# An attention-and-mixer kernel: the first block's u transposed by DMAs that ScalarE issues, the third batch's x by DMA too, key beacons loaded first

## Chip, cores and metric

The kernel runs on one core of a Trainium2 chip. The metric is device time in microseconds of one execution; the kernel before takes 357.06 us (median of 3 runs, 356.78 to 357.49). Engines: TensorE (PE, matrix multiply; PEld is its weight load), VectorE (DVE), ScalarE (ACT), GpSimd (POOL) and SyncE (SP). PE writes only PSUM, which this kernel uses as eight tiles of one bank each. Data moves by DMAs, issued from a queue of POOL, SP or ACT.

## What is computed

```
# B, H, S, Nb, D = 8, 8, 576, 16, 64
k_all = concat([beacon_k, k]); v_all = concat([beacon_v, v])
a = softmax(q @ k_all^T / sqrt(D), causal on the S part)
x = (a @ v_all) as (B, S, H*D)              # 8 x 576 x 512
h = x^T @ U @ V                             # over the 576 tokens, rank 32
u = x + h^T
out = u + relu(u @ w_ch1) @ w_ch2           # 512 -> 2048 -> 512
```

So each batch first has attention (8 heads), then its tokens are mixed (u = x + low-rank term), then each token goes through two dense layers with a residual u.

## The kernel before

**Attention.** Heads go in pairs p (4 per batch, 32 in all). For the first four batches q and k are loaded by POOL's queue into `st` tiles (`token_load`, f32 to f16 on the way; the 16 beacon rows by `key_beacons`), regrouped by DVE into `pr` (L252, and L254 for the beacons), transposed on PE (L259), and copied by DVE into `qT` and `kT` (L292, L297). Later batches are loaded whole and turned by DMA transposes that SP issues (L607). Scores (L329) go to PSUM, ACT takes the exponentials into `expt` (L335), DVE masks (L305, L307), PE multiplies by v into `po` (L357), and DVE normalises into `xb` (L365, L366): x of the batch, tokens on partitions.

**Mixing.** `mix_units` makes uT, u transposed: channels on partitions, all 4,608 tokens in a row. `head` computes x^T U (qtp, L393), `most` and `end` multiply by V (L417, L429). In the form without turning, PE also adds x itself, by matmuls of xb with an identity (`x_into`, L372), and DVE and ACT copy the result out (L406, L408). In the turned form SP first issues five DMA transposes of xb into uT (L384) and DVE adds the matmul's result to them (L404). Batch 0 has a form of its own (`first_mix`), batches 1 and 2 go without turning, batches 3 to 7 are turned.

**Dense layers.** `mlp_units` works on blocks of 512 tokens (nine). A g unit is four matmuls (L487) and a relu on ACT (L500) or DVE (L502); a c unit is four matmuls (L512), sixteen of them to an output tile of 128 tokens. At the end u must be added, with tokens on partitions again. For block 0 PE does it, by four matmuls of uT with the identity for each output tile (L520), and ACT and DVE copy alternate tiles (L527, L529) to `ob`. For blocks 1 to 8, SP issues four DMA transposes of uT into `ut` (L481) at the block's first g unit, and DVE adds `ut` on the way out (L525). SP stores `ob` (L530).

**Order.** Each engine's order is the order of the program (a manual schedule), and each engine works strictly in its own order. Dense units wait in a list, `queue`, and `fill` takes them between attention's steps. `mix(b)` puts the mixing steps of batch b among the queued units: `head` after n units, `most` after k more and `end` three later. For batches 0 and 1 the loop over `NP1` pairs runs, with `FIRST` units per pair; then `fill(AHEAD - 8)`, two `regroup_of`, `fill(8)`, and the main loop. POOL's queue is the only one that loads tokens and weights, one after another; `load_batch` issues the loads of the next batch at the first pair of a batch.

Of the kernel before, what the change touches and what calls it, by code (L numbers as in the profile page):

```python
# [18 lines left out]
P = 128  # L19
# [11 lines left out]
def kernel(  # L31
# [13 lines left out]
    nc = tc.nc  # L45
    B, H, S, D = q.shape
# [6 lines left out]
    NH2 = H // 2  # L53
# [48 lines left out]
    def pst(shape, dtype, name):  # L102
        return psum.tile(shape, dtype, tag="ps", name=name)
# [41 lines left out]
    uT = const.tile([P, NCC, B * S], F16, name="uT", tag="uT")  # L145
# [42 lines left out]
    def beacon_load(eng, src, dst, hs):  # L188
        eng.dma_start(out=dst[0:Nb], in_=src[hs].rearrange("h p d -> p h d"))  # L189

    def token_load(eng, src, dst, hs):
        eng.dma_start(out=dst[0:TP, hs, :], in_=src[hs].rearrange("h (p j) d -> p h (j d)", j=TJ))

    def key_beacons(eng, src, dst, hs):
        beacon_load(eng, src, dst[TP:TB, hs, (TJ - 1) * D : TJ * D], hs)
# [15 lines left out]
    def v_loads(src, bsrc, vs):  # L211
        v_beacon(bsrc, vs)
        v_tokens(src, vs, ALLH)
# [4 lines left out]
    ALLH = slice(0, H)  # L218
# [6 lines left out]
        return st, whole  # L225

    def emit_loads(b, L, vs):
        token_load(nc.gpsimd, k[b], L[0][0], ALLH)
        token_load(nc.gpsimd, q[b], L[0][1], ALLH)
        key_beacons(nc.gpsimd, beacon_k[b], L[0][0], ALLH)  # L230
        v_loads(v[b], beacon_v[b], vs)


# [234 lines left out]

        return head, begin, rest

    def mlp_units(t0, n, dst, flip, turned=True, last=False):


        units = []
        gT = {}
        held = {}

        def turn():
            ut = utp.tile([P, 4, DM], F16, name="ut", tag="ut")
            for cc in range(NCC):  # L480
                nc.sync.dma_start_transpose(out=ut[:, :, ts(cc, P)], in_=uT[:, cc, ds(t0, 4 * P)])  # L481
            gT["u"] = ut

        def g_part(dc, upto):
            g, done = held.get(dc) or (pst([P, 512], F32, name="gps"), 0)
            for cc in range(done, upto):
                nc.tensor.matmul(  # L487
                    g[:, 0:n], w1[:, cc, ts(dc, P)], uT[:, cc, ds(t0, n)], start=(cc == 0), stop=(cc == NCC - 1)
                )
            held[dc] = g, upto  # L490

        def g_unit(dc):
            if dc == 0:
                gT["t"] = gtp.tile([P, NDC, 512], F16, name="gT", tag="gT")
                if turned:
                    turn()
            g_part(dc, NCC)
            g, _ = held.pop(dc)
            if (dc % 3 if not turned else (dc + flip) % 2 or dc in (5, 6, 7)):
                nc.scalar.activation(out=gT["t"][:, dc, 0:n], in_=g[:, 0:n], func=AF.Relu)  # L500
            else:
                nc.vector.tensor_scalar_max(out=gT["t"][:, dc, 0:n], in0=g[:, 0:n], scalar1=0.0)  # L502

        cps = {}

        def c_unit(i, part):
            m = min(P, n - P * i)
            if part == 0:
                cps["t"] = pst([P, DM], F32, name="cps")
            ps = cps["t"]  # L510
            for dc in range(4 * part, 4 * part + 4):
                nc.tensor.matmul(  # L512
                    ps[:m, :], gT["t"][:, dc, ds(P * i, m)], w2[:, dc, :], start=(dc == 0),
                    stop=turned and dc == NDC - 1, skip_group_check=True,
                )
            if part == 3:
                ob = outp.tile([P, DM], F32, name="ob", tag="ob")
                if not turned:
                    for cc in range(NCC):
                        nc.tensor.matmul(  # L520
                            ps[:m, ts(cc, P)], uT[:, cc, ds(t0 + P * i, m)], ident, start=False, stop=True,
                            skip_group_check=True,
                        )
                if turned:
                    nc.vector.tensor_tensor(out=ob[:m, :], in0=ps[:m, :], in1=gT["u"][:m, i, :], op=ALU.add)  # L525
                elif i % 2:
                    nc.scalar.activation(out=ob[:m, :], in_=ps[:m, :], func=AF.Copy)  # L527
                else:
                    nc.vector.tensor_copy(out=ob[:m, :], in_=ps[:m, :])  # L529
                nc.sync.dma_start(out=dst(i, m), in_=ob[:m, :])  # L530

        def c_half(i, part):
            hs = ds(DM // 2 * (part // 2), DM // 2)
            if part % 2 == 0:
                cps["t"] = pst([P, DM // 2], F32, name="cph")
            for dc in range(NDC // 2 * (part % 2), NDC // 2 * (part % 2 + 1)):
                nc.tensor.matmul(  # L537
                    cps["t"], gT["t"][:, dc, ts(i, P)], w2[:, dc, hs], start=(dc == 0), stop=(dc == NDC - 1)
                )
            if part % 2:  # L540
                ob = outp.tile([P, DM // 2], F32, name="oh", tag="ob")
                nc.vector.tensor_tensor(out=ob, in0=cps["t"], in1=gT["u"][:, i, hs], op=ALU.add)
                nc.sync.dma_start(out=dst(i, P)[:, hs], in_=ob)

        units += [lambda dc=dc: g_unit(dc) for dc in range(NDC)]
        for i in range((n + P - 1) // P):
            c = c_half if last and i == n // P - 1 else c_unit
            units += [lambda i=i, part=part, c=c: c(i, part) for part in range(4)]
        return units, g_part


    good = const.tile([P, B * H, NT], F16, name="good", tag="good")
# [21 lines left out]
    rows = out.rearrange("b s c -> (b s) c")  # L574
    NP = B * NH2
    NBLK = B * S // 512
    Ls, qTs, xbs = {}, {}, {}

    def load_batch(b):
        if b < DT0:  # L580
            Ls[b] = qk_tiles()
            emit_loads(b, Ls[b], vss[b % 2])
        else:
            v_loads(v[b], beacon_v[b], vss[b % 2])
# [52 lines left out]
    def regroup_of(p):  # L637
        b, c = divmod(p, NH2)
        prs[p] = [regroup(Ls[b][0], c, i, nc.vector.tensor_copy) for i in range(2)]
# [40 lines left out]
    NF = 2  # L680
# [4 lines left out]
    LAG = 10  # L685
# [7 lines left out]
    queue = []  # L693
    state = {"t": 0}
# [13 lines left out]
    def feed(b):  # L708

        while state["t"] < NBLK and 512 * (state["t"] + 1) <= S * (b + 1):  # L710
            t = state["t"]
            units, state["part"] = mlp_units(
                512 * t, 512, lambda i, m, t=t: rows[ds(512 * t + P * i, m), :], t % 2, t > 0, t == NBLK - 1
            )
            queue.extend(units)
            state["t"] += 1

    def mix(b):

        turned = b >= NF and len(queue) >= LAG + 7  # L720
        turn, head, parts = mix_units(xbs[b], S * b, turned)
        if turned:
            turn()
        n = (LAG + 3 * (b == B - 1)) if turned else 2 if b >= NF else 0
        k = 2 if turned else 1
        most, end = parts
        rest = queue[n + k + 3 :]
        queue[:] = queue[0:n] + [head] + queue[n : n + k] + [most] + queue[n + k : n + k + 3] + [end]
        for _ in range(4):
            queue.extend(rest[:1] + [None])  # L730
            del rest[:1]
        queue.extend(rest)
        feed(b)

    with tc.manual_schedule(engines={ENG.PE, ENG.Activation, ENG.DVE, ENG.SP, ENG.Pool}):
# [11 lines left out]
        t0, sc = qkT_of(0), scores_of(0)  # L747
# [41 lines left out]
        av = av_of(2)  # L789
        head, begin, rest = first_mix(xbs[0])  # L790
        feed(0)
        part = state["part"]
        D0, D1, D2 = range(3)
        av[0]()
        head(0, 2)
# [18 lines left out]
        t0, sc = qkT_of(4), scores_of(4)  # L814
# [14 lines left out]
        for p in range(NH2, NP1):  # L829
            b, c = divmod(p, NH2)  # L830
            if c == 0:
                load_batch(b + 1)
            seq = []
            masks = lambda: None
            if p + 2 < NP1:
                seq += [lambda i=i, p=p: qkT_of(p + 2)[i]() for i in range(2)]
            if p + 3 < NP1:
                seq.append(lambda p=p: regroup_of(p + 3))
            if p + 1 < NP1:
                seq.append(sc[1])  # L840
                masks = sc[2]
            seq += av_of(p)
            sc = []
            if p + 2 < NP1:
                new_qT_of(p + 2)
                sc = scores_of(p + 2)
                seq.append(sc[0])
            seq.append(masks)
            done = 0
            for i, u in enumerate(seq):  # L850
                u()
                want = FIRST[c] * (i + 1) // len(seq)
                fill(want - done)
                done = want
            if c == NH2 - 1:
                mix(b)
# [5 lines left out]
        t0, sc, t1 = qkT_of(NP1), scores_of(NP1), qkT_of(NP1 + 1)  # L862
# [5 lines left out]
        for p in range(NP1, NP):  # L868
            b, c = divmod(p, NH2)
# [83 lines left out]
    with tc.If(n_bad != 0, label="general"):  # L953
        with tc.For_i(0, B, 1) as bi:
            L = qk_tiles()
# [13 lines left out]
            for t0 in range(0, S, 512):  # L969
                n = min(512, S - t0)  # L970
# [32 lines left out]
```

## Time and profile before

| | |
|---|---|
| median of 3 runs | 357.06 us |
| profiled execution | 356.95 us |
| its span (first to last instruction) | 355.3 us |
| DVE / ACT / POOL busy | 53% / 47% / 27% |
| granted PE clock | full in all 40 slices |
| POOL's load queue (q0) | 18.18 MB, 66.5% of 16 engines' span |
| SP's queue (q1) | 22.25 MB, 33.2% |

Busy time of an engine is the union of its instructions. A timeline line gives start, length, engine, line of the code, operation, and tiles written and read; what stands in brackets is how long the engine sat idle before it and what ended that. The share of a DMA queue is the time that its packets took, against 16 engines; it can pass 100% where an engine has several packets in flight. "To landing" is from the issue of a DMA to its completion.

### The profile page before, as it was taken

Reading aid. Unit: us, or ns where it says so; the run is one execution under the profiler, and the core shown is the slowest. Engines: PE = TensorE matmul, PEld = TensorE weight load, DVE = VectorE, ACT = ScalarE, POOL = GpSimd, SP = SyncE. Lnnn points to the kernel's source line nnn. Section 1 sums busy time; section 2 is a strip of 40 time slices with the busy share of each in tenths; the row PEclk is TensorE's granted clock in tenths of the full one; section 3 lists DMA queues with packets and bytes.
Section 4 is the critical chain, followed back from the end, with each engine's and each line's share of the span. In section 5 each row is a group of like instructions: output and inputs, shape, how many; then the busy total and the mean of one; then the engine's idle time right before and its main releaser. Section 6 shows DMA issues by size and latency. Waiting matters only on the chain.

```text
span 355.3 us, 7823 instructions
## 1 busy us (share of the span) xinstructions
PE 348.2 (98%) x3130; PEld 174.2 (49%) x3130; DVE 187.3 (53%) x482; ACT 167.4 (47%) x361; POOL 97.5 (27%) x137
## 2 busy tenths in 40 slices
PE   8999999999999999999999999999999999999995
PEld 3665555455554444444444444444454444444443
DVE  5656965588975543754455457345746522313311
ACT  5967841587654563466444664566503202301400
POOL 8956704427437048206800500000000000000000
PEclk9999999999999999999999999999999999999999
DMA  9999999999999979999999993142014413013111
GB/s 181 100 203 169 159 199 171 226 155 123 107 95 149 180 104 131 147 192 104 142 136 178 135 130 81 61 105 52 31 61 102 56 59 105 15 59 100 21 58 67
DMA packets 144170, 41.28 MB, mean 116 GB/s; under 512 B 129024, under 2 KB 139616, under 8 KB 144128
## 3 DMA queue, kind: packets, MB, share of 16 engines
q0 software_dynamic: 87440, 18.18, 66.5%
q1 hardware_dynamic: 56464, 22.25, 33.2%
q8 instruction: 26, 0.43, 0.5%
q10 hardware_dynamic: 224, 0.30, 0.3%
q14 instruction: 16, 0.13, 0.1%
HBM read 37.37 MB, written 9.44 MB: 132 GB/s over the span
## 4 chain that ended last, share of the span: by engine, by line
PE 89%; DMA 3%; DVE 2%; ACT 2%; SPq 1%; issue 0%; ACTq 0%
PE gps L487 34%; PE cps L512 32%; PE po L357 8%; PE sps L329 7%; DMA uT<-xb 2%; ACT expt L335 2%; SPq L384 1%; PE tps L259 1%; DMA stk<-in_k_dram 1%; PE cph L537 1%; PE tps L265 1%; PE ups L372 1%; PE qtp L393 1%; PE sps L321 1%; PE ups L417 1%; DVE uT L404 1%
## 5 line engine op out<-in xcount | busy, mean ns | idle before, releaser
L335 ACT ACTIVATE expt<-sps 128x496 f16<-128x496 f32 (+2 forms) x256 | 111.1, 542 | 57.6 <-PE sps L329 57.5
L487 PE MATMUL gps<-uT,w 128*128 128x512 f16 x576 | 135.7, 379 | 0.1
L512 PE MATMUL cps<-w,gT 128*128 128x512 f16 x560 | 132.7, 380 | 0.0
L500 ACT ACTIVATE gT<-gps 128x512 f16<-128x512 f32 x86 | 51.8, 607 | 94.1 <-PE gps L487 92.3
L487 PEld LDWEIGHTS <-w 128*128 128x128 f16 x576 | 51.9, 98 | 59.5 <-issue 3.8
L512 PEld LDWEIGHTS <-gT 128*128 128x128 f16 x560 | 49.9, 98 | 59.2 <-issue 6.9
L502 DVE TENSOR_SCALAR gT<-gps 128x512 f16<-128x512 f32 x58 | 40.0, 690 | 47.5 <-PE gps L487 46.7
L525 DVE TENSOR_TENSOR ob<-cps,ut 128x512 f32<-128x512 f32 x31 | 21.4, 690 | 49.6 <-PE cps L512 46.7
L207 POOL DMA_DIRECT2D vs<-in_v_dram x50 | 39.6, 809 | 21.4 <-DMA st<-in_k_dram 5.6
L357 PEld LDWEIGHTS <-expt 128*128 128x128 f16 (+1 forms) x960 | 36.2, 98 | 15.1 <-issue 2.6
L357 PE MATMUL po<-vs,expt 128*128 128x65 f16 (+1 forms) x960 | 39.4, 194 | 0.4 <-DVE expt L305 0.3
L329 PE MATMUL sps<-qT,kT 64*128 64x80 f16 (+4 forms) x384 | 34.3, 282 | 0.6 <-DVE uT L404 0.4
L366 DVE TENSOR_TENSOR xb<-po,rec 128x320 f16<-128x320 f32 x64 | 31.5, 492 | 2.2
L305 DVE TENSOR_TENSOR expt<-expt,bigmask 128x512 f16<-128x512 f16 x54 | 22.6, 419 | 11.7 <-ACT expt L335 11.7
L365 DVE RECIPROCAL rec<-po 128x5 f32<-128x5 f32 x64 | 12.0, 187 | 23.9 <-PE po L357 23.9
L329 PEld LDWEIGHTS <-kT 64*128 64x128 f16 x384 | 11.9, 94 | 22.3 <-issue 13.7
L189 POOL DMA_DIRECT2D vs<-in_beacon_v_dram x8 | 4.3, 543 | 61.4 <-PE po L357 61.4
L595 POOL DMA_DIRECT2D st<-in_q_dram x20 | 16.9, 865 | 3.3 <-DMA vs<-in_v_dram 2.2
L595 POOL DMA_DIRECT2D st<-in_k_dram x20 | 16.9, 874 | 0.9 <-DMA vs<-in_v_dram 0.9
L404 DVE TENSOR_TENSOR uT<-ups,uT 128x496 f16<-128x496 f32 x20 | 12.1, 668 | 7.5 <-PE cps L512 3.9
L292 DVE COPY qT<-tps 128x576 f16<-128x576 f16 (+1 forms) x16 | 11.8, 735 | 3.2 <-PE tps L265 2.2
L292 DVE COPY kT<-tps 128x576 f16<-128x576 f16 (+1 forms) x16 | 11.7, 734 | 2.3 <-PE tps L265 1.5
(92 smaller groups left out, 147.2 us busy)
## 6 DMA issues: line engine op xcount, KB each, us to landing
out_dram<-ob SPq DMA_DIRECT2D x35, 256.0 KB, 2.1
vs<-in_v_dram POOLq DMA_DIRECT2D x18, 128.0 KB, 7.7
w<-in_moe_w_ch_dram POOLq DMA_DIRECT2D x4, 512.0 KB, 6.1
w<-in_moe_w_ch_dram POOLq DMA_DIRECT2D x2, 1024.0 KB, 11.6
st<-in_k_dram POOLq DMA_DIRECT2D x12, 128.0 KB, 6.7
st<-in_q_dram POOLq DMA_DIRECT2D x12, 128.0 KB, 9.8
st<-in_k_dram POOLq DMA_DIRECT2D x2, 576.0 KB, 13.1
st<-in_q_dram POOLq DMA_DIRECT2D x2, 576.0 KB, 16.0
```

Of the source, the lines that this page charges most:

```text
L207: nc.gpsimd.dma_start(out=dst[a : a + nq[j], j, :, :], in_=src[hs, ds(q0[j], nq[j]), :].rearrange("h p d -> p h d"))
L292: copy(out=whole[:, :, ds(w * a, w)], in_=ps[:, 0 : TP * w].rearrange("x (j p) -> x p j", j=w),)
L305: nc.vector.tensor_tensor(out=e4, in0=e4, in1=bigmask, op=ALU.min)
L329: nc.tensor.matmul(ps[g, i][:, ds(o, w)], kT[hp, c, ds(P * ch, P)], qT[hp, c, ds(qa, w)], start=not early, stop=True, skip_group_check=early,)
L335: nc.scalar.activation(out=ex[i][:, ds(SLOT * g, gw[g])], in_=ps[g, i][:, 0 : gw[g]], func=AF.Exp, scale=scale)
L357: nc.tensor.matmul(po[:, j, :], ex[0 : nk[c], ds(blk[(c, j)], P)], vs[0 : nk[c], ds(c * H * E + h * E, E)], start=(c == 0), stop=(c == j),)
L366: nc.vector.tensor_tensor(out=xb[:, :, ds(h * D, D)], in0=po[:, :, 0:D], in1=r.broadcast_to([P, NT, D]), op=ALU.mult)
L487: nc.tensor.matmul(g[:, 0:n], w1[:, cc, ts(dc, P)], uT[:, cc, ds(t0, n)], start=(cc == 0), stop=(cc == NCC - 1))
L500: nc.scalar.activation(out=gT["t"][:, dc, 0:n], in_=g[:, 0:n], func=AF.Relu)
L502: nc.vector.tensor_scalar_max(out=gT["t"][:, dc, 0:n], in0=g[:, 0:n], scalar1=0.0)
L512: nc.tensor.matmul(ps[:m, :], gT["t"][:, dc, ds(P * i, m)], w2[:, dc, :], start=(dc == 0), stop=turned and dc == NDC - 1, skip_group_check ...
L595: nc.gpsimd.dma_start(out=dst[a : m[j], j, :, :], in_=src[:, ds(q0[j], nq[j]), :].rearrange("h p d -> p h d"))
```

## The change

Four things are edited.

- `emit_loads` issues the key beacons of a batch ahead of its k and q, where they came after both.
- Block 0 is now turned like the others: its four DMA transposes into `ut` are issued on ACT's queue (`turn_first(nc.scalar)`) at the start of the last pair of batch 1, behind the exponentials of that batch, and not at the block's first g unit. The identity matmuls (L520) go, and all four output tiles become adds on DVE (L525), where ACT had two. The relus of block 0 are shared as before (the condition now hangs on `early`).
- Batch 2 is mixed in the turned form: five DMA transposes on SP (L384), no identity matmuls (L372), and DVE adds (L404) in place of copies shared with ACT.
- With that, `head` of batch 2 comes after min(10, length of the queue less 8) units instead of 2.

```
     def emit_loads(b, L, vs):
+        key_beacons(nc.gpsimd, beacon_k[b], L[0][0], ALLH)
         token_load(nc.gpsimd, k[b], L[0][0], ALLH)
         token_load(nc.gpsimd, q[b], L[0][1], ALLH)
-        key_beacons(nc.gpsimd, beacon_k[b], L[0][0], ALLH)
         v_loads(v[b], beacon_v[b], vs)
...
-    def mlp_units(t0, n, dst, flip, turned=True, last=False):
+    def mlp_units(t0, n, dst, flip, turned=True, last=False, early=False):
...
-        def turn():
+        def turn(eng=nc.sync):
             ut = utp.tile([P, 4, DM], F16, name="ut", tag="ut")
             for cc in range(NCC):
-                nc.sync.dma_start_transpose(out=ut[:, :, ts(cc, P)], in_=uT[:, cc, ds(t0, 4 * P)])
+                eng.dma_start_transpose(out=ut[:, :, ts(cc, P)], in_=uT[:, cc, ds(t0, 4 * P)])
             gT["u"] = ut
...
-                if turned:
+                if turned and not early:
                     turn()
...
-            if (dc % 3 if not turned else (dc + flip) % 2 or dc in (5, 6, 7)):
+            if (dc % 3 if early else (dc + flip) % 2 or dc in (5, 6, 7)):
...
-        return units, g_part
+        return units, g_part, turn
...
-            units, state["part"] = mlp_units(
-                512 * t, 512, lambda i, m, t=t: rows[ds(512 * t + P * i, m), :], t % 2, t > 0, t == NBLK - 1
+            units, state["part"], state["turn"] = mlp_units(
+                512 * t, 512, lambda i, m, t=t: rows[ds(512 * t + P * i, m), :], t % 2, True, t == NBLK - 1, t == 0
             )
...
-        turned = b >= NF and len(queue) >= LAG + 7
+        turned = b >= NF
...
-        n = (LAG + 3 * (b == B - 1)) if turned else 2 if b >= NF else 0
+        n = 0 if not turned else LAG + 3 if b == B - 1 else min(LAG, len(queue) - 8)
...
-        part = state["part"]
+        part, turn_first = state["part"], state["turn"]
...
             if c == 0:
                 load_batch(b + 1)
+            if c == NH2 - 1:
+                turn_first(nc.scalar)
```

## The prediction

> **What bounds the kernel now.** I read the busy table first, then TensorE's (PE's) timeline, then VectorE's (DVE's) and the DMA issues of the stretch that the change touches.
>
> ```profile
> PE 348.2 (98%) x3130; PEld 174.2 (49%) x3130; DVE 187.3 (53%) x482; ACT 167.4 (47%) x361; POOL 97.5 (27%) x137
> ```
>
> PE works 98% of the span in an order fixed in advance, and its granted clock is full in every slice. So a microsecond of matmul that goes is a microsecond, and a microsecond in which PE waits is lost: nothing later gives it back. The sum is therefore PE work removed against new PE waits. PE's timeline prices the removed work, by the start of the group less the start of what follows (the durations shown include a pipeline drain that the next group overlaps):
>
> ```profile
> 55.95 0.39 PE L520 MATMUL cps<-ident,uT 128*128 128x128 f16 x4
> 56.18 0.31 PE L372 MATMUL uend<-ident,xb 80*128 80x80 f16 x4
> ...
> 62.40 1.03 PE L512 MATMUL cps<-w,gT 128*128 128x512 f16 x4
> 63.49 0.58 PE L329 MATMUL sps<-qT,kT 64*128 64x496 f16 x4
> ...
> 98.82 1.05 PE L372 MATMUL ups<-ident,xb 112*128 112x112 f16 x16
> 99.80 0.39 PE L417 MATMUL ups<-Vsb,qts 32*128 32x496 f16 x4
> ...
> 103.46 0.31 PE L372 MATMUL uend<-ident,xb 80*128 80x80 f16 x4
> 103.60 0.31 PE L429 MATMUL uend<-Vend,qts 128*128 128x80 f16 x4
> ```
>
> DVE's timeline shows what PE is about to need when the first block's outputs are written:
>
> ```profile
> 56.38 0.69 DVE L529 COPY ob<-cps 128x512 f32<-128x512 f32 x1 [1.64 <-PE cps L520]
> 56.99 0.48 DVE L406 CAST uT<-uend 128x320 f16<-128x320 f32 x1
> 57.39 0.34 DVE L252 COPY pr<-st 96x768 f16<-96x768 f16 x1
> 59.56 0.19 DVE L254 COPY pr<-st 16x128 f16<-16x128 f16 x1 [1.83 <-DMA st<-in_beacon_k_dram]
> 59.78 0.90 DVE L252 COPY pr<-st 96x768 f16<-96x768 f16 x2
> 60.70 0.19 DVE L254 COPY pr<-st 16x128 f16<-16x128 f16 x1
> 60.90 0.57 DVE L252 COPY pr<-st 96x768 f16<-96x768 f16 x1
> 61.47 0.76 DVE L292 COPY qT<-tps 128x576 f16<-128x576 f16 x1
> 62.60 0.76 DVE L292 COPY kT<-tps 128x576 f16<-128x576 f16 x1 [0.37 <-PE tps L259]
> 63.27 0.16 DVE L297 COPY kT<-tps 128x16 f16<-128x16 f16 x1
> ```
>
> Here, on the third batch's tokens, DVE waits 1.83 us for key beacons, and PE's scores at 63.49 start right behind the last kT copy (63.43). DVE is in order, so the first output copy stands ahead of all of it. The DMA issues say what the DMA engines are like at that time:
>
> ```profile
> q0 software_dynamic: 1175, 1.02, 127.5%
> ...
> st<-in_q_dram POOLq DMA_DIRECT2D x1, 576.0 KB, 20.6
> ...
> L481 SPq DMA_TRANSPOSE ut<-uT x4: 1241/1313/2697, 71.0 to 75.0; - x4
> DMA to landing us min/median/max: 5.8/6.6/7.5
> ```
>
> From 49 to 54 us the loads of POOL's queue alone fill the engines (share 127.5%, two packets in flight), and q of the third batch, issued at 38.55, lands 20.6 us later, at 59.15. The second block's ut transposes, issued by SP at 71, took 1.31 us each to issue and 5.8 to 7.5 us to land.
>
> **The change part by part, against the profiled run (356.95 us; span 355.3, 1.65 around it).**
>
> 1. *No identity matmuls for the first block (L520).* Each of the four groups takes 0.23 us (56.18 less 55.95; 0.23, 0.22, and 0.32 at 69.59, of which 0.09 is the switch into scores, which stays): **-0.92**. Half of it, 0.46, lies before the scores at 63.49. The last matmul group's start on the four outputs stays.
>
> 2. *Third batch by DMA transposes (L372 goes).* 99.80 - 98.82 = 0.98 and 103.60 - 103.46 = 0.14: **-1.12**. The L417 and L429 matmuls stay. Five transposes join SP's queue ahead of two outputs and of five of batch 4's kT/qT transposes; these five now go after the second output of the block instead of its first. In the profile those five were issued at 103.3 to 110.3 and took up to 6.5 us to land, and scores at 120.55 need them: 3 to 4 us to spare. The x of the batch is complete at 94.65 (the L366 behind the po of 92.64). By the new order the mixing matmuls come at about 107, so the five transposes have 12 us. Issue takes 1.4 to 1.5 each. I cost this at nothing: the value loads that fill the engines were issued until 98.2 and drain by 101.5, the next loads were issued at 104.2. DVE takes over two uT evictions that ScalarE (ACT) did, 2 x 0.67; it was busy 8.04 of 10 us there and eight PSUM buffers stand between it and PE, so from 0 to 0.5 us, taken as 0.
>
> 3. *Key beacons first.* The 1.83 us wait at 59.56 loses its cause, but q, at 59.15, is only 0.4 us earlier than the beacons. Alone that is worth at most the 0.23 us that PE waited at 63.49 (62.40 + 0.86 for four L512 to 63.49).
>
> 4. *u of the first block by ACT's transposes.* ACT ended its last relu at 49.09 and next evicts at 53.45, so it issues at once; only two evictions stand behind (L408), needed by a new PSUM tile at 62 at the earliest. No row shows ACT issuing a transpose. I take SP's 1.4 us a step under load (1.2 idle, 2.7 at worst), so the fourth starts at 49.1 + 3 x 1.4 = 53.3. Its landing is the unknown. Bounds: 5.8 us (the shortest ut row above, where the loads ran out at 75) and 9.5 us (the uT<-xb transposes of 167.6 to 173.4, beside steady loads: 7.5 / 8.6 / 9.5). I take 7.6, halfway between the two medians, since loads persist here until 65 but with larger packets: **landed at 60.9**, between 59.1 and 62.8.
>
> Now the wait. The first output add (L525, 0.61 step) needs all of ut; behind it on DVE are uend (0.40), pr k, beacons, pr q, together 2.1 us to the end of pr q: 63.0. From there to the end of the kT copy: three pr copies 0.45 + 0.22 + 0.57, the second output add 0.61 (ACT did that copy before), qT 0.76, kT 0.70, 0.16, about 3.4: 66.4. So scores come at 66.4 instead of 63.49: **+2.9**, which already has the first 0.46 of part 1 in it. The other 0.46 and part 2's 1.12 remain: 2.9 - 1.58 = **+1.3 us**. Bounds by the landing: 59.1 gives -0.5, 62.8 gives +3.2.
>
> The transposes also hold up what they pass. Alone on the engines, five of them used 45.7% of 6 us, 0.55 us each; four are 2.2 us of DMA time, taken while the engines are full, so q lands at 61.35 rather than 59.15. Then pr q ends at 61.8 and scores come at 65.2 even if ut is early: +1.7 - 1.58 = +0.1.
>
> So 356.95 + 1.3 = 358.25; the median shown is 0.11 above the profiled run: **358.4**.
>
> The Trainium skill, "DMA: Bandwidth & Descriptors", section "Queues, rings and completion order", says that each DMA engine takes turns between queues packet by packet. By it the transposes (some 470 packets each, 117 per engine) would each wait for one load packet (79 ns, 1.28 in flight, 62 ns), done about 9 us after 50, at 59; the row speaks against so prompt a start, since an output issued at 57.1 moved its first packet at 61. "Trainium Kernel Development and Optimization", section "Key Constraints", adds that issuing from several engines saves only issue time, on the same 16 engines; with that the trace agrees so far (one queue at 127.5% leaves nothing free).
>
> **Rivals.**
>
> *A, ut lands under cover (faster).* What DVE writes first is then ready before DVE comes to it, at 56.3 to 58.3. It needs the fourth transpose to land within 5 us of 53.3, and q to slip less than 1 us. For it: idle landings are 2.4 us, and kT<-st transposes have a median of 4.2. Against: the engines are full from 40 to 62. Complete cover gives -2.04 and the 0.23 of part 3: 354.8; the deciding point is about 58.3, and each microsecond after it costs one. In the middle 355.5.
>
> *B, only q's slip counts (no change).* ut is in by 59.5 but has pushed q by 2.2: +0.1, 357.2. For it: the displaced bytes are certain. Against: the landings above.
>
> *C, the third batch's transposes are late as well (slower).* Fourteen us from issue to need left PE 0.59 us idle between 180 and 190 for a later batch beside loads; here there are 12. If loads that were pushed later meet them, DVE waits 1 to 2 us at L404 with masks and kT copies behind: 359.5 to 360.3. Against: the gap in the loads from 101.5 to 104.
>
> That the new adds do not take effect is no rival: the new order of PE's instructions has 36 matmuls fewer and they are in it nowhere else.
>
> **Chances.** Forecast 0.43 (356.6 to 360.2 by its landing bounds, the part under 357.8 being counted with B), B 0.23, A 0.27, C 0.07. About 0.2% (0.7 us) is what a measurement of this kernel can tell from no change. Faster by more: A, 0.27. Within: B, 0.23. Slower: forecast and C, 0.50. The range must take in most of A and the late landings: 354.9 to 360.0. The forecast's own is 357.8 to 360.0.
>
> **What would show it.** Right: in the new profile the first L525 waits for a DMA (ut<-uT), ends around 61.5, and PE is idle 2 to 4 us between 60 and 67; ACT's L481 rows start near 49.1. B shows itself by DVE waiting for q's DMA before an L252. A shows itself by PE at 98% and more with no wait there, and the blocks after 110 us starting 2 us earlier. I am wrong if transposes under full load land in under 5 us, if ACT issues them much earlier or later than 49.1, or if PE stays fed by other work while DVE waits.

## The result, and the profile after

The changed kernel takes **362.88 us** (median of 6 runs, 361.59 to 364.97) against 357.37 (356.78 to 359.75) for the kernel before beside it: ratio 1.0147, 95% interval [1.0105, 1.0188]. That is 5.5 us slower; the forecast was 358.4 and its range ended at 360.0. The profiled execution took 362.77 us, with a span of 361.1 (before: 355.3).

The page of the changed kernel: the busy table, TensorE's granted clock in 40 slices of 9 us, and the chain of work that ended last.

```profile
PE 348.6 (97%) x3094; PEld 173.1 (48%) x3094; DVE 189.5 (52%) x486; ACT 165.1 (46%) x357; POOL 97.7 (27%) x137
...
PEclk9999999699999999999999999999999999999999
...
PE 91%; DMA 3%; ACT 2%; DVE 1%; ACTq 1%; issue 0%; DVEq 0%
```

PE lost its 36 matmuls, yet it is busy 0.4 us longer in a span that is 5.8 us longer. Two things are new: one slice with a clock of 0.6, from 63 to 72 us, and a DMA on the chain (its row by lines names it: DMA ut<-uT, 3%). PE's timeline of the changed kernel shows the place (start, duration, operation; in brackets the idle time before it and who ended it):

```profile
56.10 0.31 PE L372 MATMUL uend<-ident,xb 80*128 80x80 f16 x4
...
56.40 4.48 PE L512 MATMUL cps<-w,gT 128*128 128x512 f16 x20
66.40 0.66 PE L259 MATMUL tps<-ident,pr 96*128 96x96 f16 x6 [5.52 <-DVE pr L252]
66.86 1.91 PE L512 MATMUL cps<-w,gT 128*128 128x512 f16 x4
68.56 0.70 PE L259 MATMUL tps<-ident,pr 96*128 96x96 f16 x6
69.05 1.91 PE L512 MATMUL cps<-w,gT 128*128 128x512 f16 x4
70.90 0.61 PE L329 MATMUL sps<-qT,kT 64*128 64x496 f16 x4
71.44 1.04 PE L512 MATMUL cps<-w,gT 128*128 128x512 f16 x4
```

PE stands still for 5.52 us, from 60.88, and is slow when it goes on: four L512 take 1.91 us where the last row has 1.04. The scores, at 63.49 before, come at 70.90, 7.4 us late. DVE's timeline of the same stretch says what PE waited for:

```profile
53.63 1.26 DVE L406 CAST uT<-ups 128x496 f16<-128x496 f32 x2 [1.85 <-PE ups L417]
64.37 0.69 DVE L525 TENSOR_TENSOR ob<-cps,ut 128x512 f32<-128x512 f32 x1 [9.47 <-DMA ut<-uT]
64.97 0.48 DVE L406 CAST uT<-uend 128x320 f16<-128x320 f32 x1
65.37 0.35 DVE L252 COPY pr<-st 96x768 f16<-96x768 f16 x1
65.75 0.21 DVE L254 COPY pr<-st 16x128 f16<-16x128 f16 x1
65.99 0.98 DVE L252 COPY pr<-st 96x768 f16<-96x768 f16 x2
...
69.97 0.15 DVE L297 COPY kT<-tps 128x16 f16<-128x16 f16 x1
```

DVE idles 9.47 us for ut, and the copies that PE needs are queued behind that add. Nothing behind it waits for its own loads any more: they have all landed by then. The last of them is the third batch's q, issued at 39.34 and landed 22.8 us later, at 62.1 (before: 59.15). ACT's timeline, then the trace's rows on line L481 (the duration of one issue, minimum, median and maximum, then first and last start), with the DMA issues of 38 to 66 us last (median from issue to landing):

```profile
48.65 0.60 ACT L500 ACTIVATE gT<-gps 128x512 f16<-128x512 f32 x1 [0.27 <-PE gps L487]
48.66 7.46 ACTq L481 DMA_TRANSPOSE ut<-uT  x4
56.16 1.06 ACT L408 ACTIVATE uT<-ups 128x496 f16<-128x496 f32 x2 [6.91 <-issue]
```

```profile
L481 ACTq DMA_TRANSPOSE ut<-uT x4: 1303/1610/2815, 48.7 to 53.3; - x4
...
DMA to landing us min/median/max: 2.3/2.4/11.1
```

```profile
ut<-uT ACTq DMA_TRANSPOSE x4, 11.0
st<-in_beacon_k_dram POOLq DMA_DIRECT2D x2, 16.0 KB, 12.9
```

The fourth transpose is issued at 53.3, as forecast, and lands 11.0 us later at 64.3, where 60.9 was forecast. The DMA traffic of the changed kernel from 52 to 64 us, in 40 slices of 0.3 us, with the load queue (q0) and ACT's queue (q10):

```profile
GB/s 203 198 201 194 194 152 139 189 192 191 192 186 189 189 188 179 150 197 234 186 169 102 23 16 9 144 177 168 167 147 162 157 132 134 130 154 143 155 155 129
...
q0 software_dynamic: 3487, 1.35, 106.3%
q10 hardware_dynamic: 2176, 0.52, 47.3%
```

The first transposed packet moves at 52.6. From then on the two queues move packet for packet: 186 and 190 (q0 and q10) from 54 to 55 us, 200 and 198 in the next, 359 and 361 from 61 to 62. So the last transposed packet comes only after about as many packets of loads. In between, from 58.6 to 59.5, almost nothing moves (9 to 23 GB/s). Every run with these transposes has such a hole of about 1 us, and in this stretch the kernel before has none (lowest slice 117 GB/s). No view says what opens it.

Finally PE's clock by stretches of the changed kernel (length, busy time of PE, PEld, DVE, ACT, POOL, granted clock, DMA share with 1.00 for one packet in flight on each engine, GB/s):

```profile
56.00:60.00 4.00, 4.00 (x27) 1.96 (x25) 0.00 (x0) 1.06 (x2) 0.53 (x1) 1.00 1.48 138
60.00:64.00 4.00, 0.88 (x5) 0.20 (x2) 0.00 (x0) 0.00 (x0) 1.53 (x2) 1.00 1.83 149
64.00:66.40 2.40, 0.00 (x1) 0.01 (x1) 1.97 (x6) 0.00 (x0) 0.98 (x3) 0.54 3.59 139
66.40:69.00 2.60, 2.60 (x16) 1.50 (x17) 2.38 (x5) 0.00 (x0) 1.71 (x3) 0.50 1.89 152
69.00:71.00 2.00, 2.00 (x10) 0.61 (x9) 0.83 (x2) 0.00 (x0) 2.00 (x3) 0.50 1.22 257
71.00:73.00 2.00, 2.00 (x16) 0.89 (x15) 0.49 (x1) 1.66 (x4) 0.21 (x1) 1.00 1.22 256
```

The clock halves at about 64.2, 3.3 us after PE fell idle, and is back some 4.6 us after PE resumed. From L259 (66.40) to the scores (70.90) PE needs 4.50 us; before it was 2.48 (61.01 to 63.49). The Trainium skill, "TensorE: Matmul & The Clock Gate", section "Part 1: The HAM clock gate (the "warmup" mystery)", states this: half clock after an idle window of about 3.4 us, full clock after about as long a busy one. The trace agrees on the fall (3.3 us) and is a little longer on the return (4.6).

**Where the time went**, as the start in the changed kernel less the start of the same matmuls before: +0.15 at 39.80 (ahead of the change), -0.30 at 60.15 (identity matmuls gone), +5.39 at L259, +7.41 at the scores, +7.13 at 94.59, +6.92 at 116.54 (the third batch's mixing is past), +5.67 at 185.47, and +5.8 in the span. All of the loss lies between 60.9 and 71 us; 1.7 us come back later. Most of that, 1.25 us, comes back at one place behind 182 us, where PE waits for DVE in the kernel before:

```profile
182.83 0.38 PE L329 MATMUL sps<-qT,kT 64*128 64x496 f16 x2
183.41 0.35 PE L329 MATMUL sps<-qT,kT 64*128 64x464 f16 x1 [0.20 <-DVE uT L404]
183.99 0.35 PE L329 MATMUL sps<-qT,kT 64*128 64x464 f16 x1 [0.23 <-DVE uT L404]
184.28 1.04 PE L512 MATMUL cps<-w,gT 128*128 128x512 f16 x4
185.47 0.61 PE L357 MATMUL po<-vs,expt 128*128 128x65 f16 x15 [0.16 <-DVE ob L525]
```

From the first to the fourth row takes 1.45 us here and 0.52 in the changed kernel, the next step 1.19 and 0.87. Counted from start to start these waits cost more than the idle times in brackets, which begin only at the end that the view gives the matmul before.

### The profile page after: what moved, and what is told of

Its sections match the earlier page's. It is cut to its first block, busy times and chain, and to the rows that moved or that the text cites. A ratio compares the mean times of both kernels' runs of the same rounds, so it can differ in the third digit from the quotient of the medians.

```text
span 361.1 us, 7770 instructions
## 1 busy us (share of the span) xinstructions
PE 348.6 (97%) x3094; PEld 173.1 (48%) x3094; DVE 189.5 (52%) x486; ACT 165.1 (46%) x357; POOL 97.7 (27%) x137
## 4 chain that ended last, share of the span: by engine, by line
PE 91%; DMA 3%; ACT 2%; DVE 1%; ACTq 1%; issue 0%; DVEq 0%
PE gps L487 35%; PE cps L512 33%; PE po L357 8%; PE sps L329 8%; DMA ut<-uT 3%; PE tps L259 2%; ACT expt L335 2%; PE idle L239 1%; ACTq L481 1%; PE cph L537 1%; PE tps L265 1%; PE qtp L393 1%; PE sps L321 1%; PE ups L417 1%; PE qtp L445 0%; DVE kT L292 0%
## 5 line engine op out<-in xcount | busy, mean ns | idle before, releaser
L512 PE MATMUL cps<-w,gT 128*128 128x512 f16 x560 | 134.1, 383 | 0.0
L512 PEld LDWEIGHTS <-gT 128*128 128x128 f16 x560 | 50.3, 98 | 60.4 <-issue 8.3
L525 DVE TENSOR_TENSOR ob<-cps,ut 128x512 f32<-128x512 f32 x35 | 24.2, 690 | 59.4 <-PE cps L512 49.3
L329 PE MATMUL sps<-qT,kT 64*128 64x80 f16 (+4 forms) x384 | 34.2, 282 | 0.7 <-DVE uT L404 0.3
L329 PEld LDWEIGHTS <-kT 64*128 64x128 f16 x384 | 11.9, 94 | 22.9 <-issue 13.7
L404 DVE TENSOR_TENSOR uT<-ups,uT 128x496 f16<-128x496 f32 x24 | 14.5, 667 | 5.7 <-PE ups L417 5.7
L259 PE MATMUL tps<-ident,pr 96*128 96x96 f16 x126 | 9.7, 220 | 5.5 <-DVE pr L252 5.5
L259 PEld LDWEIGHTS <-pr 96*128 96x128 f16 x126 | 8.0, 105 | 11.5 <-DVE pr L252 7.3
```

Source lines behind the costliest of these rows:

```text
L259: return [lambda ps, o, n, j, t=t: nc.tensor.transpose(ps[:, ds(o, n)], t[:n, j, :, :], ident[:n, :n]) for t in pr]
L329: nc.tensor.matmul(ps[g, i][:, ds(o, w)], kT[hp, c, ds(P * ch, P)], qT[hp, c, ds(qa, w)], start=not early, stop=True, skip_group_check=early,)
L512: nc.tensor.matmul(ps[:m, :], gT["t"][:, dc, ds(P * i, m)], w2[:, dc, :], start=(dc == 0), stop=turned and dc == NDC - 1, skip_group_check ...
```

## The experiments

**Theory after the result.** The four transposes of block 0 run beside a load stream that, in the kernel before, leaves the DMA engines no gap before 65 us. They land last and hold the in-order DVE, and the idle time then costs PE its clock. **Rivals.** The one that the expectations call rival 2: who waits for ut hardly matters; the transposes take DMA time from loads that PE needs, wherever they are put. Two others: the loss is in the third batch's transposes or the new order of the beacons; or it is ACT, blocked for 7.46 us by its issues.

### Part by part: e1_u_only, e2_x_only, e3_beacons_only

Each has one part of the change alone: e1 ACT's transposes for block 0, e2 the third batch's transposes, e3 the beacons first.

```diff
 e2, on the kernel before
-        turned = b >= NF and len(queue) >= LAG + 7
+        turned = b >= NF
-        n = (LAG + 3 * (b == B - 1)) if turned else 2 if b >= NF else 0
+        n = 0 if not turned else LAG + 3 if b == B - 1 else min(LAG, len(queue) - 8)
```

> Only the first block's u is turned by transposes on ScalarE's queue; third batch and key beacons stay as before. Theory (DVE is held at the first output add by ut's landing, PE runs dry for 5.5 us and then works 4.5 us at half clock): nearly all of the loss is here, +6 to +7 us against before, with the same idle time before L259 and the same half clock behind it. Rival 1 (the loss comes from the third batch's mixing): within 1 us of before. Rival 2 (the transposes' DMA time delays the loads, whatever waits for ut): DVE's wait ends with a load of q and not with ut.

> Only the third batch is mixed in the turned form (20 identity matmuls less); first block and beacons as before. Theory: a small gain, -0.2 to -1.4 us: 1.1 us of matmul go, some 0.6 us of PE waits at L329 behind DVE's adds come, and a wait of 1.2 us in batch 4 may go or stay. Rival 1: slower by 1 us or more.

> Only the key beacons are issued ahead of k and q. Theory: 0 to -0.3 us, since q, which the same copies need, lands only some 0.4 us before the beacons did; DVE's wait of 1.8 us becomes one for q of about 1.5. If beacons were what PE waited for, -0.5 us or more.

Beside a kernel before of 356.84 us: e1 **363.73** (ratio 1.0182 [1.0157, 1.0207]), e2 **355.79** (0.9957 [0.994, 0.9975]), e3 **356.86** (1.0002 [0.9987, 1.0018]). So e1 costs 6.9, e2 gives 1.05 and e3 nothing; the sum, +5.85, is the whole change (+5.5). The loss is in block 0 alone. PE's waits in e2 show that its gain is not simply the matmuls that it removes:

```profile
108.19 0.39 PE L329 MATMUL sps<-qT,kT 64*128 64x336 f16 x6
108.78 0.25 PE L329 MATMUL sps<-qT,kT 64*128 64x208 f16 x1 [0.20 <-DVE qT L292]
109.36 0.25 PE L329 MATMUL sps<-qT,kT 64*128 64x208 f16 x1 [0.34 <-DVE uT L404]
109.54 2.76 PE L512 MATMUL cps<-w,gT 128*128 128x512 f16 x12
```

DVE, with two more evictions, now makes PE wait there: these eight matmuls take 1.35 us from start to start, where they took 0.41 before (at 97.54). So 0.94 of the 1.12 us is lost again on the spot, and from 100 to 117 us e2 gains only 0.2. The rest of its gain is the waits behind 182 us, of which none is left in e2's trace (1.1 us less). They are not tied to the third batch: they shrink to 0.6 us in e12 and vanish in e9, which mix it as before. What decides them is open.

### Earlier, and from another engine: e4_sp_early, e5_sp_same

Both are the whole change with SP as the issuer; e4 issues once the first batch's mixing is done, e5 keeps the place in the program.

```diff
 e4
         rest(3, 1, V)
+        turn_first(nc.sync)
...
-            if c == NH2 - 1:
-                turn_first(nc.scalar)
 e5
-                turn_first(nc.scalar)
+                turn_first(nc.sync)
```

> The whole change, but the first block's transposes are issued by SP as soon as the block's uT is complete (near 26 us; SP issues nothing else from 20 to 57). Theory (only the landing of ut against DVE's add counts): ut is there by 40, DVE and PE do not wait, no half clock, -1 to -2.4 us against before (355 to 356.4). Rival 2 (the 2.2 us of DMA time count, since the loads are backed up until 65 wherever the transposes go): q of the third batch still lands near 61.5 and PE waits 1 to 2 us before L259, so 357 to 359.

> The whole change, but SP issues the first block's four transposes at the same place in the program (SP waits for nothing there that ScalarE does not wait for, so they may go out as early as the block's uT is complete). Theory (landing decides, the issuing engine does not): if SP issues them near 26 us, as with the early issue before, 357 to 359 us with PE waiting for w1 near 38; if near 49, as the changed kernel, 362 to 364. Rival (ScalarE's own issue, 7.5 us for four, is what is slow): clearly better than the early issue by SP.

e4: **357.82** (1.002 [0.9998, 1.0042]); e5: **357.7** beside 357.0 (1.0026 [1.001, 1.0041]). SP has nothing before them and issued them at 23.3 and 23.1 us, so e5 did not show the engine at ACT's time: it repeats e4. They landed 9.0 to 9.3 us (e4) and 8.6 to 9.4 us (e5) after their issue, beside loads as well: slow landing does not need ACT as the issuer. Issued 25 us earlier, ut is there long before DVE needs it. That wins back 5 us, but not the 2 that the removed work should have given. PE's and then DVE's timeline of e4 show why:

```profile
39.39 1.04 PE L487 MATMUL gps<-uT,w 128*128 128x512 f16 x4 [1.59 <-DMA w<-in_moe_w_ch_dram]
```

```profile
58.10 0.69 DVE L525 TENSOR_TENSOR ob<-cps,ut 128x512 f32<-128x512 f32 x1 [1.42 <-PE cps L512]
...
62.39 0.63 DVE L252 COPY pr<-st 96x768 f16<-96x768 f16 x2 [2.67 <-DMA st<-in_q_dram]
```

The first weights, just in time before, are now 1.59 us late, and q of the third batch is late again, at 62.4 instead of 59.15. This is rival 2: the DMA time is missed wherever it is taken. It leaves PE 1.9 us behind the kernel before at 118 us, and 0.6 behind 185 us; the 1.26 between are the waits behind 182 us, which e4 no longer has.

### The clock: e6_warm

The changed kernel with idle matmuls on the identity, thrown away, in PE's wait.

```diff
-        fill(8)
+        fill(6)
+        keep_warm(pst([P, 512], F32, name="idle"), 23)
+        fill(2)
```

> The changed kernel with 23 idle 128x512 matmuls (5.0 us of PE work on the identity, into a PSUM tile that nobody reads) in the place where PE stood idle before L259. Theory (the idle time halves PE's clock for the next 4.5 us, which costs 2.0 us by itself): no half clock, the wait for ut stays, -1.5 to -2.2 us against the changed kernel, so near 361 us or +4 to +5 against before. Rival (the slow 4.5 us come from the DMA or from DVE): no better than the changed kernel.

**361.43** beside 357.0 (1.014 [1.011, 1.0169]). In the profiled run the clock is 1.0 throughout:

```profile
66.17 0.43 PE L259 MATMUL tps<-ident,pr 96*128 96x96 f16 x6 [0.61 <-DVE pr L252]
...
69.76 0.58 PE L329 MATMUL sps<-qT,kT 64*128 64x496 f16 x4 [1.17 <-DVE kT L297]
```

The scores come 1.14 us earlier than in the changed kernel (69.76 for 70.90), of which 0.22 is an earlier ut (64.15 for 64.37). So the halved clock costs about 0.9 us and not the 2.0 that PE's rows suggest: at full speed PE waits 1.17 us for DVE's kT instead. The two ratios overlap; only the traces show this difference.

### What the transposes cost when nobody reads them: e8_unread, e9_unread_warm, e12_unread_warm12

The kernel before, with ACT issuing the four transposes into a ut that nobody reads. e9 and e12 add 23 and 12 idle matmuls in the place of e6.

```diff
 e8, on the kernel before
+            if c == NH2 - 1:
+                turn_first(nc.scalar)
 e12, on e8
-        fill(8)
+        fill(6)
+        keep_warm(pst([P, 512], F32, name="idle"), 12)
+        fill(2)
```

> The kernel before, with the four transposes of the first block's u added on ScalarE's queue at the changed kernel's place, but read by nobody: identity matmuls, copies, third batch and beacons as before. What is left is the DMA and issue time alone. Theory (most of the loss is DVE's wait for ut itself): q of the third batch lands 1.5 to 2.5 us later, +1.0 to +2.5 us, no half clock. Rival 2 (delayed loads explain the loss whoever reads ut): +5 us or more.

> The kernel before with the four transposes that nobody reads, and 23 matmuls on the identity (128x512, 5 us of PE time at full rate, also thrown away) put where PE otherwise waits for the third batch's q. If the loss of 4 us with the unread transposes is the displaced loads plus PE's halved clock, the clock stays at 1.0 here, the wait for q and the beacons stays (PE's scores of the third batch late by about 2.5 us against the kernel before), and the time is 358.6 to 359.8. If the clock is no cause of its own (the displaced loads alone cost the 4 us), 360.5 to 361.5. If the idle matmuls themselves stand in the way, above 361.5.

> The same as the run before it (kernel before, four unread transposes, idle matmuls in PE's wait) with 12 idle matmuls in place of 23: 2.6 us, which end at about 62.8 and so before the third batch's beacons land, instead of 1.3 us after them. If displaced loads and the halved clock share the 4 us of the unread transposes, the clock stays at 1.0, PE's wait for the third batch is covered, the shift at the scores is 2.4 to 3.4 us and the time 359.2 to 360.2. If the clock has no part in it, 360.6 to 361.2 as without the idle matmuls. If 2.6 us of idle work is too little to keep the clock up, the granted clock falls to a half behind the wait and the time is 360.6 or more.

e8 took **360.95** beside 357.0 (1.0117 [1.0093, 1.0141]), far more than the theory allowed and less than the 5 us of rival 2: nobody waits for ut and still 4 us are gone. PE's timeline of e8, and its clock:

```profile
63.39 0.43 PE L259 MATMUL tps<-ident,pr 96*128 96x96 f16 x6 [1.93 <-DVE pr L252]
63.66 1.03 PE L512 MATMUL cps<-w,gT 128*128 128x512 f16 x4
...
64.79 1.82 PE L512 MATMUL cps<-w,gT 128*128 128x512 f16 x4
```

```profile
64.00:66.00 2.00, 2.00 (x14) 0.86 (x11) 1.99 (x5) 0.00 (x0) 0.98 (x2) 0.72 2.16 189
66.00:68.00 2.00, 2.00 (x8) 0.41 (x7) 0.04 (x1) 0.83 (x2) 1.34 (x2) 0.50 1.91 227
```

The beacons, behind q in the queue, land at 62.7 (before: 59.5), PE waits 1.93 us, and the clock halves at about 64.9, although PE is at work again: that is 3.5 us after PE fell idle (61.46). e9 took **361.1** (1.0126 [1.0109, 1.0143]). Its clock stayed full, but the 23 idle matmuls ended at 65.08, 1.3 us after DVE went on with the beacons (63.79 in that run), and held the next work up: it prices nothing. e12, with 12, took **360.14** beside 357.01 (1.0095 [1.0078, 1.0112]):

```profile
60.39 2.75 PE L239 MATMUL idle<-ident 128*128 128x512 f16 x12
62.98 1.03 PE L512 MATMUL cps<-w,gT 128*128 128x512 f16 x4
63.85 0.42 PE L259 MATMUL tps<-ident,pr 96*128 96x96 f16 x6
...
66.56 0.58 PE L329 MATMUL sps<-qT,kT 64*128 64x496 f16 x4 [0.30 <-DVE kT L297]
```

PE is covered, its clock is full, and the scores are 3.07 us late (66.56 for 63.49). DVE works without a pause from the beacons (63.16) to the kT copy that the scores wait for, so the idle matmuls do not set their start. So the displaced loads alone cost **3.1 us**. The bytes say the same: from 52 to 64 us the loads moved 1.91 MB in the kernel before and 1.35 in the changed one, and the 0.56 MB between are 3.1 us at the 182 GB/s of before (an estimate). The clock costs the 0.8 between e12 and e8, which their traces confirm: the scores start together (66.56 and 66.54), and at the next L520 e8 is 0.77 behind (68.72 for 67.95). The beacons came 0.4 us earlier in e8 than in e12, so both costs hold to some tenths only.

### Fewer loads in front: e10_light, e11_light_before

```diff
-            emit_loads(b, Ls[b], vss[b % 2])
+            emit_loads(b, Ls[b], vss[b % 2], slice(0, H // 2) if b == 2 else ALLH)
```

> The changed kernel, but of the third batch's k and q only the first four heads are loaded (GpSimd writes zeros for the others), so 576 KB less goes through POOL's load queue between 40 and 62 us; its output for that batch is another. At some 200 GB/s that is 2.9 us less in front. If ut lands late because the transposes share full DMA engines with the loads ahead, the last transpose lands at 61 to 62 instead of 64.3, q at about 59, PE's wait falls from 5.5 to 2 to 3 us and the time is 358.5 to 361. If the landing is the transposes' own pace (8 to 11 us behind an issue that takes 7.5), it stays at 64 and the time within 1 us of 362.9. If the value loads that follow move up and fill the engines just as much, ut stays at 63.5 to 64.5 too while q comes 3 us earlier: ut alone then makes the wait.

> The kernel before with the same four heads left out of the third batch's loads, as the base for the run beside it. PE waits there for next to nothing at that place, so the time should be 356.3 to 357.0, 0 to 0.4 below the kernel before. If it is more than 1 us faster, the load stream bounds the kernel before already.

e10: **361.77** beside 356.79 (1.0151 [1.0128, 1.0175]); e11: 1.0049 [1.0007, 1.009], 356.54 in its profiled run. The lighter stream does not speed up the kernel before. In e10 (its line numbers are 3 higher) ut is 1.1 us earlier and PE's wait 1.0 shorter:

```profile
63.22 0.69 DVE L528 TENSOR_TENSOR ob<-cps,ut 128x512 f32<-128x512 f32 x1 [8.75 <-DMA ut<-uT]
```

```profile
65.44 0.43 PE L262 MATMUL tps<-ident,pr 96*128 96x96 f16 x6 [4.53 <-DVE pr L255]
```

576 KB less in front bring the landing forward by 1.1 us and not by 2.9. The value loads moved up: from 52 to 64 us POOL's queue moved 5495 packets here and 3487 in the changed kernel. They are smaller packets (1.18 and 1.35 MB), but they fill the queue more (163.2% and 106.3% of 16 engines). That is nearest to the third case of the expectation: q lands at 58.4, long before ut, and the landing of ut alone makes PE's wait of 4.53 us. So a backlog in front explains 1.1 us of the late landing at most. That the loads beside the transposes are the cause is what the packet counts say (turn for turn, above), and the later transposes of the changed kernel, beside few loads, landed in 2.3 to 4.7 us (median 2.4, from 230 us on). No run has ACT's transposes without loads beside them.

### The gain alone: e7_x_later

The third batch's transposes alone, as in e2, with its mixing matmuls later in the order: nine units of the queue go ahead of them, where e2 has at most eight.

```diff
-        n = (LAG + 3 * (b == B - 1)) if turned else 2 if b >= NF else 0
+        n = 0 if not turned else LAG + 3 if b == B - 1 else 9 if b == NF else LAG
```

> Third batch by transposes alone, as before, but its mixing stands one dense unit later (9 units ahead of head), so that the four mixing tiles come behind the second visit of scores and not ahead of it. Theory (the 0.6 to 0.9 us that this edit gives back are PE waiting for PSUM tiles that DVE's four adds hold): 0.3 to 0.9 us better than with 8 units (355.8), so 354.9 to 355.5. Rival (the adds delay the masks and the kT copy instead): no better, or worse.

**355.53** beside 357.0 (0.9959 [0.9946, 0.9972]), better than both kernels; against e2 the intervals do not tell it apart. The L329 waits of e2 are gone, and one of 0.32 us for ACT (at 109.07) is left; from 100 to 117 us it gains 0.5 where e2 gains 0.2, each in one trace.

## Why the prediction was wrong, point by point

The direction and the mechanism were as forecast: DVE waits for ut in front of the third batch's copies, and PE stands still for them. The size was wrong, and PE's clock was left out of the sum. The premise that nothing later gives back lost time did not hold either: waits of a later batch gave back 1.25 us.

- *Identity matmuls, -0.92*: gone as forecast. The part before the scores (0.46) shows at 60.15 (from +0.15 to -0.30) and is then lost in the wait; of the other half 0.28 shows behind the scores.
- *Third batch, -1.12*: the number was right (e2: -1.05), by luck. The DVE wait that I bounded by 0 to 0.5 and took as 0 costs 0.94, and some 1.1 us of waits that I had not counted vanish later. Rival C is out: in the changed kernel the adds (L404) wait for PE and never for a transpose.
- *Beacons, at most 0.23*: right (e3: nothing).
- *Issue by ACT*: right. The fourth starts at 53.3; that it is so to the tenth is luck, since the first went out 0.4 earlier than I had it and the three steps took 1.5 instead of 1.4. ACT is blocked until 56.1 and its uT eviction (L408) starts at 56.16, but PE goes on without an idle row until 60.88: that ACT is held up costs nothing there.
- *Landing after 7.6 us, at 60.9*: **the step that failed.** It took 11.0, so 64.3, outside my bounds of 59.1 to 62.8. I had bounded it with transposes beside loads that were running out or steady (5.8 to 9.5). Here the load queue had 1.06 packets in flight on each engine from 52 to 64 us, beside the transposes all the way and taking every other turn, and about 1 us of the 3.4 is the hole from 58.6 to 59.5. The 3.4 us more go straight through: 1.3 + 3.4 = +4.7.
- *DVE's chain, 2.1 and 3.4*: 64.37 to L259 at 66.40 is 2.03, right. On to the end of kT (70.12) it is 3.7, 0.49 of it waiting for the slow PE. PE's clock was missing from my sum: 0.9 us by e6. With it +5.6; the profiled run shows +5.8. The terms behind the scores agree only in sum: -1.58 forecast, -1.74 measured, of which 1.25 are the later waits.
- *Displaced DMA time, 2.2 us*: too small. e12 measures 3.1, and so do the bytes. My 0.55 each came from transposes without loads beside them. In the changed kernel from 52 to 64 us ACT's queue has 47.3% of 16 engines' time, so 0.473 x 12 = 5.7 us, against 2.2, and the loads run beside it. So B ("only q's slip", 357.2) was priced too low: even with ut early the slip would have cost 3.1 - 2.04 = +1.1, about 358.
- *Rival A*, cover: out. e4 has the cover, and does not get faster, because q is late.

I set the rule of the Trainium skill ("DMA: Bandwidth & Descriptors", "Queues, rings and completion order": turns by packet) against a row and got 59 by it. The trace agrees with the turns: the two queues move packet for packet (186 and 190, 200 and 198 in a microsecond). The estimate left out what the runs add: the first transposed packet moved at 52.6, 3.9 us after its issue and not at 50, there were 544 packets to a transpose and not 470, each has a time of its own (5.7 x 16 us over 2176 packets, 42 ns), and there is the hole of about 1 us.

Together: of the 6.9 us of e1, 3.1 are the displaced loads (e12), about 0.9 the clock (e6, e12 to e8), and the remaining 2.9 the wait for ut itself, with the 0.92 of removed work already taken off. The last is a difference, not measured alone. Still open is what makes the hole in the DMA traffic, and what decides the waits behind 182 us.

## What to carry to other kernels

Work moved from a busy engine to the DMAs is free only where the DMA engines have gaps: ask what is already in the queues at that moment, and price the move by the loads it displaces as well as by its own landing. A result that lands late should not be the first thing that an in-order engine needs in front of other work. An idle time of some microseconds on PE can cost more than its length, when the clock falls and the work behind it runs at half speed: 0.9 us more here, behind 5.5 idle. And a wait priced by the idle time in a timeline can be priced too low: in e2, 0.54 us in brackets were 0.94 from start to start.

## What the runs showed of the hardware that was not expected

- Transposes beside a full load queue: first packet 3.9 us after issue, landing 8.4 to 11.1 us after it, where the later ones of the same kernel, with few loads beside them, have a median of 2.4. A packet's time is 42 ns beside loads, 35 without the stretch from 58 to 59.6; from 300 to 340 us, without them, the same kind of queue (SP's, outputs included) has 21.1% of 16 x 40 us for 5124 packets, 26 ns.
- Beside these transposes the whole DMA traffic all but stops once, for about 1 us: 9 to 23 GB/s from 58.6 to 59.5 in the changed kernel, and the same in all nine runs that issue them beside loads (10 GB/s or less at the bottom). The kernel before, e2 and e3 have no such hole from 52 to 64 us (lowest slices 117, 104 and 113).
- Issuing blocks the engine: four issues hold ACT for 7.46 us (6.76 to 7.79 in e1, e6, e8, e9 and e12, 6.11 in e10), and SP for 5.9 to 6.0 under load (e4, e5) and 5.14 without (302.50 and 330.12 in the changed kernel).
- PE's clock halved in e8 after only 1.93 us idle, 1.5 us after PE had resumed, and by the mean clocks not in every run: three of six have 0.993 to 0.994 (361.5 to 362.7 us), three 0.997 to 0.999 (360.1 to 360.4). Not all of that gap is the clock: in the profiled one, at 361.5, the waits behind 182 us take 1.1 us more than in e12. e4's 1.59 us idle left it at 1.0 in the profiled run. The section of the Trainium skill named above speaks of an idle window of about 3.4 us that runs freely; that 1.93 us can be enough it does not say, and no run here shows what decides it.
